# TensorE in source order in the second mixer, and a finer-stepped spectral mixing

## The chip, the cores and the metric

The kernel runs on one core of a Trainium2 chip. The time is device microseconds of one execution. The kernel before took 2022.99 us (median of 3 runs, 2015.35 to 2023.32). A core has TensorE (PE, with weight loads as PEld), VectorE (DVE), ScalarE (ACT), GpSimd (POOL) and SyncE (SP), whose queue issues nearly all DMAs here. Each engine works through its own queue in order, and engines wait for each other by semaphores.

## The reference

Attention over pooled keys and values, then a mixer with a low-rank mixing of the tokens, then a second mixer whose token mixing is the real part of a two-dimensional Fourier transform:

```python
attn_out = softmax(q @ pooled_k.T / 8) @ pooled_v      # 8 x 8 heads x 576 x 64
u  = x + (x.T @ U @ V).T                               # first mixer, 8 x 576 x 512
x1 = u + relu(u @ w_ch1) @ w_ch2                       # 512 -> 2048 -> 512
u2 = x1 + real(fft(fft(x1, axis=1), axis=2))           # second mixer
un = (u2 - mean(u2)) / sqrt(var(u2) + 1e-6)
out = u2 + relu(un @ moe2_w_ch1) @ moe2_w_ch2
```

All matrix products are made from pairs of rounded halves (high and low), so each is three matmuls.

## The kernel before

**The stages.** The first mixer works on 18 blocks of 256 tokens (16 slots a block); beside it run generators, called lanes, each of which does a little work per `step`: attention for the coming sequences, the conversion of the weights, and, once these are done, lane `d`, the spectral mixing of the eight sequences (`Dft.run`, in groups of 1, 2, 3 and 2 sequences). The second mixer works on 9 blocks of 512 tokens with 8 passes a block, called pairs here, since each takes two 128-column groups of the hidden layer: 72 pairs. Between its parts a `tick` steps all lanes, four times a pair. Lane `p` (`prep_a`) prepares the next block: it loads four tiles `ul` of the mixed sums, normalizes them (statistics on DVE, L762), transposes them on PE (L775), and splits them into operands `x`.

**A pair.** The first product of the mixer is made in seven sub-products of 256 x 256 x 256 (`product`, six matmuls of 256 columns each), of tiles `wr`, which hold two products each and come through a ring of four tiles from DRAM (`ring_load`). They go to the two halves of PSUM banks `h0` (`u`) and `h1` (`y`, `v`). In source order: s1 into `v`, a11 into `u`, s2 added to `u`, s4 added to `v`, a12 into `y`, s3 added to `u`, a22 added to `u`. ACT copies a half to `side` whenever the value so far is needed (L1157, L1159, L1166: s1, a11, and a11 + s2). DVE then adds `side` to both halves of `h1` (L103), ACT makes `hh` (relu, L1139) and DVE `hl` (L1140): that is the low half of the hidden layer; the high half follows from s3 and a22. `st2_a` multiplies these by the second weight: a group of six matmuls of 512 columns for each of four token tiles, into banks `o0`, `o1`, `hu`, `m`. Tiles 0 and 1 need the low half of the same pair, tiles 2 and 3 the high half of the pair before.

**A sequence of the spectral mixing.** For each of three row ranges it loads `F` and `R` (SP), forms sums and differences on POOL (`S`) and DVE (`R`, `E`), and splits them on ACT (`xh`, `xe`) and DVE. Then come five groups of matmuls with the table `st`, and two or three with `dt`, in banks `s0` and `s1`, with the sums stored to DRAM as `u2d`. Its `yield`s set how the work falls on steps: 17 a sequence, 19 for the last one of a group.

**What sets the order.** A scheduler orders PE, DVE, POOL and SP by a simulated timeline. ACT is in source order from the second block of the first mixer on (`order.enter_context`).

Of the kernel before, what the change touches and what calls it, by code (L numbers as in the profile page):

```python
# [38 lines left out]
NRING = 4  # L39
# [5 lines left out]
def kernel(  # L45
# [28 lines left out]
    mhalf = const.tile([128, 1], F32, name="mhalf")  # L74
    nc.vector.memset(mhalf, -0.5)
    W = {}
    state = {"n": 0, "free": False, "m": "s1", "u": 0, "slot": 0, "x1": 0, "u2": 0, "op": 0, "banks": ("s0", "s1", "hu")}

    def scratch(i, w=1024, dt=F32):

# [9 lines left out]
    def bank(tag):  # L90
        return ps_b.tile([128, 512], F32, tag=tag, name=tag)
# [10 lines left out]
    def add(eng, o, a, b):  # L102
        eng.tensor_tensor(out=o, in0=a, in1=b, op=ALU.add)  # L103
# [5 lines left out]
    def mm(o, a, b, start, stop):  # L109
        nc.tensor.matmul(o, a, b, start=start, stop=stop, skip_group_check=True)  # L110
# [393 lines left out]
    class Dft:  # L504
# [12 lines left out]
            self.cat = None  # L517

        def pbank(self):
            self.n += 1  # L520
            return bank(state["banks"][self.n % len(state["banks"])])

        def run(self, b, group):
            p1 = self.p
            z = b * S
            slot = b - group[0]

            def tl(tag, shape=(128, DM), dt=F32):
                return p1.tile(list(shape), dt, tag=tag, name=tag)
# [22 lines left out]
            fr = loads(0)  # L552
            yield
            yield
            X, XE = [], []
            for i in range(3):
                f, r, n = fr
                s = tl("S")
                e = tl("E")
                add(nc.gpsimd, s[:n], f[:n], r[:n])  # L560
                sub(nc.vector, r[:n], f[:n], r[:n])
                nc.gpsimd.tensor_copy(e[:n, 0:1], s[:n, 0:1])
                nc.gpsimd.memset(e[:n, 511:512], 0.0)
                sub(nc.vector, e[:n, 256:511], r[:n, 1:256], r[:n, 256:511])
                add(nc.vector, e[:n, 1:256], s[:n, 1:256], s[:n, 256:511])
                c2 = s[:n, 511:512].to_broadcast([n, 64])
                xe = tl(f"xe{i}", (128, 96 if i < 2 else 64), F32R)
                if i < 2:
                    xh, xl = tl(f"xh{i}", dt=F32R), tl(f"xl{i}", dt=F32R)
                    split(xh, xl, e)  # L570
                    nc.scalar.activation(out=xe[:, 0:64], in_=c2, func=ACTF.Copy)
                    sub(nc.vector, xe[:, 64:96], c2[:, 0:32], xe[:, 0:32].bitcast(F32))
                    X.append((xh, xl))
                    XE.append(xe)
                else:
                    m = self.sm
                    for h, y, w in ((xe, c2, 64), (None, e, 512)):
                        h = h or tl("S", dt=F32R)
                        q = r[:, 0:w]
                        nc.vector.tensor_scalar(out=q[:n], in0=y[:n], scalar1=m[:n, 0:1], scalar2=None, op0=ALU.mult)  # L580
                        nc.scalar.activation(out=h[:n], in_=y[:n], func=ACTF.Copy)
                        nc.vector.scalar_tensor_tensor(out=h[:n], in0=h[:n].bitcast(F32), scalar=m[:n, 1:2], in1=q[:n], op0=ALU.mult, op1=ALU.add)
                    X.append((h,))
                    XE.append(xe)
                    yield
                if i < 2:
                    fr = loads(i + 1)
                    yield
                yield
            P = []  # L590
            if slot == 0:
                self.cat = (tl("cath", (128, 4, 99), F32R), tl("catl", (128, 4, 99), F32R), tl("catp", (96, 99), F32R))
# [12 lines left out]
            for c in range(2):  # L605
                for g in range(2):
                    m = 127 if c and g else 128
# [17 lines left out]
            for i in range(3 if b == group[-1] else 2):  # L625
                f, r = tl("F"), tl("R")
                if i < 2:
                    k0, n = KT[i]
                    ks = slice(k0, k0 + n)
                    Q = [(ph[:m, ks], pl[:m, ks], m) for ph, pl, m in P]  # L630
                    qx = px[:, ks]
                    nc.sync.dma_start(out=f[:n], in_=x1d[z + k0:z + k0 + n, :])
                    mirror_in(r, i)
                else:
                    n = 33 * len(group)
                    hi, lo, qx = self.cat
                    Q = [(hi[:p[2], a, :n], lo[:p[2], a, :n], p[2]) for a, p in enumerate(P)]
                    qx = qx[:, :n]
                    for j, zj in enumerate(y * S for y in group):
                        nc.sync.dma_start(out=f[33 * j:33 * j + 33], in_=x1d[zj + 256:zj + 289, :])  # L640
                        nc.sync.dma_start(out=r[33 * j:33 * j + 32], in_=x1d[zj + 544:zj + 576, :])
                        nc.sync.dma_start(out=r[33 * j + 32:33 * j + 33], in_=x1d[zj + 288:zj + 289, :])
                yield
                yield
                a, bb = bank("s0"), bank("s1")
                for c, o in ((0, a), (1, bb)):
                    for g in range(2):
                        ph, pl, m = Q[2 * c + g]
                        th, tl_ = self.dt[:m, c, g, 0], self.dt[:m, c, g, 1]
                        last = c == 1 and g == 1  # L650
                        mm(o[:n, 0:NL], ph, th, g == 0, False)
                        mm(o[:n, 0:NL], ph, tl_, False, False)
                        mm(o[:n, 0:NL], pl, th, False, last)
                mm(a[:n, 0:NL], qx, self.pt, False, True)
                s, e = tl("S"), tl("E")
                nc.scalar.activation(out=e[:n, 0:NL], in_=bb[:n, 0:NL], func=ACTF.Copy)
                sub(nc.vector, s[:n, 0:257], a[:n, 0:257], e[:n, 0:257])
                add(nc.vector, e[:n, 0:257], a[:n, 0:257], e[:n, 0:257])
                add(nc.gpsimd, f[:n, 0:256], f[:n, 0:256], s[:n, 0:256])
                add(nc.vector, f[:n, 256:512], f[:n, 256:512], e[:n, 1:257])  # L660
                add(nc.vector, r[:n, 0:256], r[:n, 0:256], e[:n, 0:256])
                add(nc.gpsimd, r[:n, 256:512], r[:n, 256:512], s[:n, 1:257])
                if i < 2:
                    nc.sync.dma_start(out=u2d[z + k0:z + k0 + n, :], in_=f[:n])
                if i == 0:
                    for a, m in ((1, 15), (16, 112)):
                        nc.sync.dma_start(out=u2d[z + 288 + a:z + 288 + a + m, :], in_=r[a:a + m])
                elif i == 1:
                    nc.sync.dma_start(out=u2d[z + 416:z + 544, :], in_=r)
                else:  # L670
                    for j, zj in enumerate(y * S for y in group):
                        nc.sync.dma_start(out=u2d[zj + 256:zj + 289, :], in_=f[33 * j:33 * j + 33])
                        nc.sync.dma_start(out=u2d[zj + 544:zj + 576, :], in_=r[33 * j:33 * j + 32])
# [54 lines left out]
    def tbank():  # L728
        if state["free"] and len(pools) == 1:
            return bank("m")  # L730
        state["n"] += 1
        return bank(("s0", "s1")[state["n"] % 2])
# [11 lines left out]
    def prep_a(b):  # L744
# [11 lines left out]
        for t in range(TA // 128):  # L756
            u = us.pop(t)
# [12 lines left out]
            nc.vector.tensor_tensor(out=rs[:, 0:1], in0=rs[:, 0:1], in1=rs[:, 1:2], op=ALU.mult)  # L770
            nc.vector.tensor_scalar(out=u, in0=u, scalar1=mv[:, 0:1], scalar2=rs[:, 0:1], op0=ALU.subtract, op1=ALU.mult)
            yield
            o = tbank()
            for k in range(KD):
                nc.tensor.transpose(o[:, k * 128:k * 128 + 128], u[:, k * 128:k * 128 + 128], ident)  # L775
# [49 lines left out]
    def product(n, o, x, first):  # L825
        w = wring[n // 2][:, n % 2].rearrange("p h (k c) -> p h k c", k=2)
        for k in range(2):
            for a, y in ((0, 0), (0, 1), (1, 0)):
                mm(o, w[:, a, k], x[:, y, k], first and k == 0 and a == y == 0, False)
        if n % 2:  # L830
            del wring[n // 2]
            ring_load(n // 2 + NRING)

    def st1(js, f, tag):
        beside = len(js) == 1 and df is not None
# [136 lines left out]
    def step(name):  # L972
        g = lanes.get(name)
        if g is not None and next(g, 1):
            del lanes[name]
# [75 lines left out]
    for gi, js in enumerate(groups):  # L1051
# [5 lines left out]
        for f in range(NF):  # L1057
# [35 lines left out]
            for i in range(2 if wide else 1):  # L1093
                slot += 1
                if wide or slot % 4:
                    step("a")
                if slot % 4 != 3:
                    step("d")
                if prev and i < len(prev[0]):
                    st2(prev[0][i], prev[1], prev[2][i], tags[i])  # L1100
                for name in ("p", "mix", "w", "prep"):
                    step(name)
                if last:
                    step("p")
# [41 lines left out]
            step(name)  # L1146

    prev = None
    for b in range(NBA):
        for p in range(NPR):  # L1150
            x = ops[b]
# [46 lines left out]
            rest_a(b, t)  # L1198
    for t in range(2, TA // 128):
        st2_a(prev, t)  # L1200
    order.close()
    dbx.close()

# [101 lines left out]
```

## Time and profile before

| | |
|---|---|
| profiled execution | 2017.55 us |
| its span | 2015.8 us |
| PE busy, share of the span | 93% |
| PEld / DVE / ACT / POOL busy | 82% / 50% / 33% / 13% |
| granted PE clock, mean | 0.979 |
| DMA moved | 335.62 MB, mean 166 GB/s |

Busy times of matmuls overlap, since they are pipelined: a matmul of 256 columns shows 0.28 us and the next starts 0.12 us later. So the spacing of starts tells PE's pace, and the busy share doesn't. A releaser is what ended the idle time before an instruction, inferred from semaphore events; "issue" is put where the profile shows none.

### The profile page before, as it was taken

What the parts mean: (1) busy time and instruction counts of PE and PEld (TensorE: products, weight loads), DVE (VectorE), ACT (ScalarE), POOL (GpSimd) and SP (SyncE); (2) the same over time, 40 slices, a digit from 0 to 9 for tenths busy, and PEclk for the clock granted to TensorE, in tenths of its full rate; (3) what the DMA queues carried; (4) which work ended last, traced back from release to release, by engine and by line L of the source; (5) the groups of instructions that cost most, each with busy time, mean ns of one, the idle gap of its engine ahead of it and who ended that gap; (6) DMA issues with size and microseconds to landing.
All of it is one profiled execution on the core that took longest, in us unless ns stands there. A gap on an engine that the chain in (4) does not pass through costs nothing.

```text
span 2015.8 us, 30975 instructions
## 1 busy us (share of the span) xinstructions
PE 1874.7 (93%) x11252; PEld 1653.4 (82%) x11252; DVE 1002.7 (50%) x2285; ACT 674.7 (33%) x2116; POOL 258.5 (13%) x389
## 2 busy tenths in 40 slices
PE   4789999999999999999997898999999999998998
PEld 4578889888888888888886787888888888887887
DVE  7985464555544445455457545543434343434322
ACT  6553444344333322232234332322232323222321
POOL 3430111111100001112114312210000000000000
PEclk9799999999999999999999899999999999999999
DMA  9445464645635345223226556574656565656563
GB/s 362 154 135 152 139 213 131 195 156 165 194 106 154 92 138 146 76 65 104 79 82 217 191 167 234 196 240 157 209 170 207 166 206 179 191 177 198 166 221 126
DMA packets 255416, 335.62 MB, mean 166 GB/s; under 512 B 84576, under 2 KB 109248, under 8 KB 255264
## 3 DMA queue, kind: packets, MB, share of 16 engines
q1 hardware_dynamic: 254336, 330.25, 52.3%
q0 software_dynamic: 928, 3.40, 0.5%
q8 instruction: 89, 1.46, 0.3%
q14 instruction: 63, 0.52, 0.1%
HBM read 268.69 MB, written 64.88 MB: 165 GB/s over the span
## 4 chain that ended last, share of the span: by engine, by line
PE 63%; DMA 9%; DVE 5%; ACT 2%; issue 2%; POOL 1%; SPq 1%; DVEq 0%; POOLq 0%; ACTq 0%
PE h L110 29%; PE o L110 20%; PE hu L110 5%; PE m L110 4%; PE s L110 4%; DMA cv<-w2b 4%; DMA R<-x1d 1%; ACT side L1166 1%; DMA ud<-x 1%; DMA raw<-vr 1%; PE s L775 1%; DMA F<-x1d 1%; POOL S L103 0%; DVE hl L876 0%; ACT s L413 0%
## 5 line engine op out<-in xcount | busy, mean ns | idle before, releaser
L110 PE MATMUL h<-utx,w 128*128 128x256 f32 (+1 forms) x3048 | 477.6, 301 | 14.0 <-DVE hl L876 7.5
L110 PE MATMUL h<-x,wr 128*128 128x256 f32 x3024 | 430.3, 290 | 54.8 <-ACT side L1166 32.6
L110 PEld LDWEIGHTS h<-x,wr 128*128 128x128 f32 x3024 | 405.4, 194 | 89.1 <-ACT side L1166 46.1
L110 PEld LDWEIGHTS h<-utx,w 128*128 128x128 f32 x3048 | 431.1, 191 | 54.4 <-DVE hl L876 10.6
L110 PE MATMUL o<-w,hh 128*128 128x512 f32 x1632 | 473.4, 402 | 1.6 <-ACT hh L875 1.1
L110 PEld LDWEIGHTS o<-w,hh 128*128 128x128 f32 x1632 | 296.6, 192 | 53.2 <-ACT hh L875 2.7
L110 PE MATMUL o<-w,hl 128*128 128x512 f32 x816 | 268.9, 396 | 1.9 <-DVE hl L876 1.9
L103 DVE TENSOR_TENSOR side<-h,side 128x512 f32<-128x512 f32 (+1 forms) x144 | 79.2, 555 | 239.7 <-ACT side L1166 221.4
L110 PEld LDWEIGHTS o<-w,hl 128*128 128x128 f32 x816 | 148.0, 189 | 26.0 <-DVE hl L876 3.2
L1159 ACT ACTIVATE side<-h 128x256 f32<-128x256 f32 x72 | 27.6, 384 | 302.4 <-PE h L110 302.4
L413 ACT ACTIVATE s<-s,mx 128x72 f32<-128x72 f32 x296 | 90.7, 333 | 68.2 <-DVE mx L410 67.7
L870 ACT ACTIVATE low<-h 128x256 f32<-128x256 f32 x102 | 39.2, 384 | 218.5 <-PE h L110 162.4
L1139 ACT ACTIVATE hh<-side 128x512 fp32r<-128x512 f32 (+1 forms) x144 | 74.3, 521 | 81.2 <-DVE side L103 76.8
L100 DVE TENSOR_TENSOR x<-ul,x 128x256 fp32r<-128x256 f32 x112 | 43.6, 423 | 114.3 <-ACT x L106 114.3
L875 ACT ACTIVATE hh<-h 128x256 fp32r<-128x256 f32 x170 | 65.8, 387 | 94.9 <-PE h L110 86.3
L103 DVE TENSOR_TENSOR low<-h,low 128x256 f32<-128x256 f32 x102 | 42.9, 420 | 102.0 <-ACT hh L871 99.4
L876 DVE SCALAR_TENSOR_TENSOR hl<-h,hh 128x256 fp32r<-128x256 f32 x170 | 70.7, 416 | 32.6 <-ACT hh L875 32.0
L100 POOL TENSOR_TENSOR wo<-wo 128x256 fp32r<-128x256 f32 x56 | 43.4, 786 | 324.0 <-ACT wo L106 309.5
L766 POOL TENSOR_TENSOR rs<-mv,mhalf 128x1 f32<-128x1 f32 x36 | 20.9, 586 | 493.9 <-DVE mv L765 492.8
L110 PE MATMUL m<-w,hh 128*128 128x512 f32 x304 | 82.4, 390 | 0.0
L1140 DVE SCALAR_TENSOR_TENSOR hl<-side,hh 128x512 fp32r<-128x512 f32 (+1 forms) x144 | 77.6, 562 | 4.0 <-ACT hh L1139 3.5
L110 PE MATMUL hu<-w,hh 128*128 128x512 f32 x288 | 77.8, 392 | 1.3 <-ACT hh L1139 1.3
(254 smaller groups left out, 2446.9 us busy)
## 6 DMA issues: line engine op xcount, KB each, us to landing
wr<-wc SPq DMA_DIRECT2D x252, 512.0 KB
x<-x SPq DMA_DIRECT2D x56, 256.0 KB
wc<-wo SPq DMA_DIRECT2D x56, 256.0 KB
ur<-ud SPq DMA_DIRECT2D x36, 256.0 KB
x1d<-ur SPq DMA_DIRECT2D x36, 256.0 KB
ul<-u2d SPq DMA_DIRECT2D x36, 256.0 KB
ur<-u2d SPq DMA_DIRECT2D x36, 256.0 KB
out<-ur SPq DMA_DIRECT2D x36, 256.0 KB
```

What stands on the lines that cost most here:

```text
L100: eng.tensor_tensor(out=o, in0=a, in1=b, op=ALU.subtract)
L103: eng.tensor_tensor(out=o, in0=a, in1=b, op=ALU.add)
L110: nc.tensor.matmul(o, a, b, start=start, stop=stop, skip_group_check=True)
L413: nc.scalar.activation(out=s[:n, a], in_=v[:, k], func=ACTF.Exp, bias=mx[:n, a:a + 1], accum_out=sm[:n, a:a + 1])
L766: nc.gpsimd.tensor_tensor(out=rs[:, 0:1], in0=v, in1=mhalf, op=ALU.pow)
L775: nc.tensor.transpose(o[:, k * 128:k * 128 + 128], u[:, k * 128:k * 128 + 128], ident)
L870: nc.scalar.activation(out=low, in_=o[:, T:2 * T], func=ACTF.Copy)
L875: nc.scalar.activation(out=hh, in_=p, func=ACTF.Relu)
L876: nc.vector.scalar_tensor_tensor(out=hl, in0=p, scalar=0.0, in1=hh.bitcast(F32), op0=ALU.max, op1=ALU.subtract)
L1139: nc.scalar.activation(out=hh[:, i], in_=c, func=ACTF.Relu)
L1140: nc.vector.scalar_tensor_tensor(out=hl[:, i], in0=c, scalar=0.0, in1=hh[:, i].bitcast(F32), op0=ALU.max, op1=ALU.subtract)
L1159: nc.scalar.activation(out=side[:, 0], in_=u, func=ACTF.Copy)
```

## The change

Four edits. PE is put in source order from the start of the second mixer (`manual_schedule`). The spectral mixing gets more `yield`s (26 steps a sequence, 31 for the last of a group), asks for the next `F` and `R` one step ahead of the split, waits a step more ahead of the matmuls, and splits each last part in three steps; lane `d` is stepped in every slot of the first mixer instead of three of four. While a spectral sum is in banks `s0` and `s1`, a flag holds the transposes of lane `p` back, and both draw banks from one counter. `product` puts the request for a new weight tile one product later.

```diff
         def pbank(self):
-            self.n += 1
-            return bank(state["banks"][self.n % len(state["banks"])])
+            state["n"] += 1
+            return bank(state["banks"][state["n"] % len(state["banks"])])
...
             fr = loads(0)
+            yield
             yield
             yield
...
                 xe = tl(f"xe{i}", (128, 96 if i < 2 else 64), F32R)
+                if i < 2:
+                    fr = loads(i + 1)
+                yield
                 if i < 2:
                     xh, xl = tl(f"xh{i}", dt=F32R), tl(f"xl{i}", dt=F32R)
                     split(xh, xl, e)
...
                     yield
-                if i < 2:
-                    fr = loads(i + 1)
-                    yield
-                yield
+                yield
+            yield
...
                 yield
                 yield
+                yield
+                state["busy"] = True
                 a, bb = bank("s0"), bank("s1")
...
                 mm(a[:n, 0:NL], qx, self.pt, False, True)
+                yield
                 s, e = tl("S"), tl("E")
...
                 add(nc.gpsimd, r[:n, 256:512], r[:n, 256:512], s[:n, 1:257])
+                yield
+                state["busy"] = False
                 if i < 2:
                     nc.sync.dma_start(out=u2d[z + k0:z + k0 + n, :], in_=f[:n])
...
             yield
+            while state["busy"]:
+                yield
             o = tbank()
             for k in range(KD):
                 nc.tensor.transpose(o[:, k * 128:k * 128 + 128], u[:, k * 128:k * 128 + 128], ident)
...
                 mm(o, w[:, a, k], x[:, y, k], first and k == 0 and a == y == 0, False)
+        if state["late"] is not None:
+            ring_load(state["late"])
+            state["late"] = None
         if n % 2:
             del wring[n // 2]
-            ring_load(n // 2 + NRING)
+            state["late"] = n // 2 + NRING
...
-                if slot % 4 != 3:
-                    step("d")
+                step("d")
...
     prev = None
+    chain = ExitStack()
+    chain.enter_context(tc.manual_schedule(engines={mybir.EngineType.PE}))
     for b in range(NBA):
```

How rows move. PE in the middle of the sixth block, before: the first six-matmul rows of `h0` are a11; those of `h1` with `x2_16728` and `x2_16196` are s4 and a12; `h0` with `x2_16694` is s2, with `x2_16474` s3, with `x2_16363` a22; `h1_17340` is the next pair's s1. `hu`, `m` and `o0` are the groups of the second product.

```order
L110 MATMUL h0_17225<-x2_16193,wr_17110 128x256 x6
L110 MATMUL hu_16898<-w_771,hl_17205 128x512
L110 MATMUL hu_16898<-w_841,hl_17205 128x512
L110 MATMUL h1_17226<-x2_16728,wr_17144 128x256 x6
L110 MATMUL h1_17226<-x2_16196,wr_17159 128x256 x6
L110 MATMUL m_16937<-w_771,hl_17205 128x512
L110 MATMUL m_16937<-w_841,hl_17205 128x512
L110 MATMUL h0_17225<-x2_16694,wr_17144 128x256 x6
L110 MATMUL h0_17225<-x2_16474,wr_17159 128x256 x6
L110 MATMUL h1_17340<-x2_16475,wr_17202 128x256 x6
L110 MATMUL h0_17225<-x2_16363,wr_17202 128x256 x6
L110 MATMUL o0_16854<-w_937,hh_17278 128x512 x2
```

PE in a pair of the seventh block, now: `h0` with `x2_17555` is s2, `h1` s4 and a12, `h0` with `x2_17335` s3.

```order
L110 MATMUL hu_17759<-w_423,hl_17729 128x512
L110 MATMUL hu_17759<-w_469,hl_17729 128x512
L110 MATMUL h0_17741<-x2_17555,wr_17676 128x256 x6
L110 MATMUL h1_17742<-x2_17587,wr_17691 128x256 x6
L110 MATMUL h1_17742<-x2_17057,wr_17691 128x256 x6
L110 MATMUL m_17796<-w_423,hh_17728 128x512 x2
L110 MATMUL m_17796<-w_469,hh_17728 128x512 x2
L110 MATMUL m_17796<-w_423,hl_17729 128x512
L110 MATMUL m_17796<-w_469,hl_17729 128x512
L110 MATMUL h0_17741<-x2_17335,wr_17726 128x256 x6
L110 MATMUL o0_17713<-w_488,hh_17792 128x512 x2
L110 MATMUL o0_17713<-w_488,hl_17793 128x512
```

Between s2 and s3 there are now two products and a group of six wide matmuls, where there was nothing.

DVE at the end of the fifth block, before: the residual adds of that block (`ur`), the statistics of the next block's first two tiles (BN_STATS), and the add of `side` of the pair that runs then.

```order
L103 TENSOR_TENSOR ur_16781<-hu_16039,ur_16781 128x512
L762 BN_STATS bs_16977<-ul_16905 128x6
L103 TENSOR_TENSOR ur_16783<-m_16078,ur_16783 128x512
L762 BN_STATS bs_17073<-ul_16907 128x6
L763 BN_AGGR mv_16978<-bs_16977 128x2
L103 TENSOR_TENSOR side_11744<-h1_16786,side_11744 128x512
```

DVE at the same place, now.

```order
L103 TENSOR_TENSOR ur_16781<-hu_16041,ur_16781 128x512
L103 TENSOR_TENSOR side_11609<-h1_16786,side_11609 128x512
L769 BN_STATS bs_16977<-ul_16907 128x6
L769 BN_STATS bs_17073<-ul_16909 128x6
L103 TENSOR_TENSOR ur_16783<-m_16078,ur_16783 128x512
L770 BN_AGGR mv_16978<-bs_16977 128x2
L1151 SCALAR_TENSOR_TENSOR hl_16836<-side_11609,hh_16835 128x512
```

The add of `side` has gone ahead of the two statistics instructions; the `hl` that follows it stands behind them.

## Rows read from the trace of the kernel before

**Rows 1.** Busy times by window: span, engines with counts, PE clock, DMA share, GB/s

```profile
1350.00:2012.00 662.00, 622.49 (x3763) 551.92 (x3762) 247.99 (x609) 176.43 (x442) 14.10 (x24) 0.98 0.58 185
1550.00:1600.00 50.00, 48.54 (x299) 43.09 (x298) 19.34 (x48) 13.97 (x34) 1.10 (x2) 1.00 0.53 166
```

**Rows 2.** PE's waits, 1093 to 2016 us: total us, times, longest us

```profile
PE h L110 <- ACT side L1166: 32.6, 56, 7.0
PE h L110 <- issue: 14.6, 6, 3.2
PE s L110 <- DVE S L582: 6.9, 1, 6.9
PE s L110 <- ACT xh L106: 3.8, 1, 3.8
PE h L110 <- DVE low L103: 2.5, 1, 2.5
```

**Rows 3.** Timeline of a steady pair: start us, us, engine line op [idle before <-releaser]

```profile
1519.85 2.48 PE L110 MATMUL h<-x,wr 128*128 128x256 f32 x18 [0.47 <-ACT side L1166]
...
1522.17 2.00 PE L110 MATMUL o<-w,hh 128*128 128x512 f32 x8
...
1526.73 1.36 PE L110 MATMUL h<-x,wr 128*128 128x256 f32 x10
1527.92 0.63 PE L110 MATMUL hu<-w,hl 128*128 128x512 f32 x2
...
1529.80 0.86 PE L110 MATMUL h<-x,wr 128*128 128x256 f32 x6
1530.70 0.38 ACT L1166 ACTIVATE side<-h 128x256 f32<-128x256 f32 x1 [1.58 <-PE h L110]
...
1531.13 1.70 PE L110 MATMUL h<-x,wr 128*128 128x256 f32 x12 [0.47 <-ACT side L1166]
```

**Rows 4.** Groups by form, 1350 to 2000 us: count | busy us, mean ns | idle before

```profile
L1140 DVE SCALAR_TENSOR_TENSOR hl<-side,hh 128x512 fp32r<-128x512 f32 x55 | 38.0, 692 | 0.8 <-ACT hh L1139 0.4
L103 DVE TENSOR_TENSOR side<-h,side 128x512 f32<-128x512 f32 x55 | 37.9, 688 | 202.9 <-ACT side L1166 202.9
L1139 ACT ACTIVATE hh<-side 128x512 fp32r<-128x512 f32 x55 | 34.8, 632 | 54.4 <-DVE side L103 53.5
...
L775 PE MATMUL s<-ident,ul 128*128 128x128 f32 x96 | 13.4, 272 | 0.0
```

**Rows 5.** Timeline at the end of a block

```profile
1631.87 1.26 SPq L929 DMA_DIRECT2D out<-ur  x2
...
1635.01 0.93 SPq L750 DMA_DIRECT2D ul<-u2d  x2
...
1637.61 0.69 DVE L762 BATCH_NORM_STATS2 bs<-ul 128x6 f32<-128x512 f32 x1 [0.86 <-DMA ul<-u2d]
...
1638.81 0.68 DVE L762 BATCH_NORM_STATS2 bs<-ul 128x6 f32<-128x512 f32 x1
...
1639.49 0.99 DVE L103 TENSOR_TENSOR side<-h,side 128x512 f32<-128x512 f32 x2
...
1640.25 1.67 PE L110 MATMUL h<-x,wr 128*128 128x256 f32 x12 [1.62 <-issue]
```

**Rows 6.** Timeline of a spectral sequence beside the second mixer

```profile
1140.05 1.09 SPq L537 DMA_DIRECT2D R<-x1d  x3
...
1147.62 0.63 ACT L106 ACTIVATE xh<-E 128x512 fp32r<-128x512 f32 x1 [7.78 <-DVE E L100]
...
1148.72 4.21 PE L110 MATMUL h<-x,wr 128*128 128x256 f32 x18 [6.95 <-ACT side L1166]
...
1154.20 0.63 ACT L106 ACTIVATE xh<-E 128x512 fp32r<-128x512 f32 x1 [2.62 <-DVE E L100]
...
1162.43 0.63 ACT L581 ACTIVATE S<-E 99x512 fp32r<-99x512 f32 x1 [1.51 <-DVE R L580]
```

More of the change, by code (lines that the diff above doesn't have):

```diff
@@ L76 @@
     W = {}
-    state = {"n": 0, "free": False, "m": "s1", "u": 0, "slot": 0, "x1": 0, "u2": 0, "op": 0, "banks": ("s0", "s1", "hu")}
+    state = {"n": 0, "free": False, "m": "s1", "u": 0, "slot": 0, "x1": 0, "u2": 0, "op": 0, "busy": False, "late": None, "banks": ("s0", "s1", "hu")}
     def scratch(i, w=1024, dt=F32):
@@ L1200 @@
         st2_a(prev, t)
+    chain.close()
     order.close()
```

## The prediction

> **What bounds the kernel now.** I read the busy shares by window first, then TensorE's list of waits, then the timeline at the places which that list names. The windows [rows 1] split the second mixer in two. From 1350 us on it is periodic: 56 of its 72 pairs in 662 us, with TensorE busy for 622 of them, VectorE for 248 and ScalarE for 176, and the DMA engines at 58%. So TensorE's own work and its waits set the pace there, and nothing else is near full. Before 1350 us the same pairs share TensorE with the last spectral sequences. The list of waits [rows 2] has one large entry: 56 waits, 32.6 us, for ScalarE's copy `side` (L1166), then 14.6 us under "issue", then single long ones (6.9, 3.8, 2.5 us).
>
> The timeline of one pair [rows 3] shows what the 56 are. TensorE ends six matmuls of `h`, ScalarE copies that result from 1530.70 to 1531.08, and only then do the next matmuls of `h` start, at 1531.13: 0.47 us idle. In the order of before the s2 product is followed at once by the s3 product, which adds to the same PSUM half; s3 has to wait until s2's value has been copied out. It costs more than 0.47 us. A pair lasts 11.28 us (1519.85 to 1531.13). Ten matmuls of 256 columns take 1.19 us (1526.73 to 1527.92), 0.119 each. From 1522.17 to 1529.80, 7.63 us, there are 24 matmuls of 512 columns and 18 of 256: 18 x 0.119 = 2.14, so 24 take 5.49, 0.229 each. A pair of 42 and 24 without a wait is 5.00 + 5.49 = 10.49 us. So each wait costs 0.79 us: the idle time, the last matmul's drain and the slow restart.
>
> The "issue" waits are no issue. At the end of a block [rows 5] VectorE holds two statistics instructions that need the next block's `ul`, asked for at 1635.01 and used at 1637.61; the add of `side` sits behind both, at 1639.49, and TensorE's products, which overwrite what that add reads, start at 1640.25. VectorE's queue is the cause.
>
> The long waits are the spectral mixing [rows 6]: `R` is asked for at 1140.05, the sums of it are ready for ScalarE's `xh` at 1147.62 after 7.78 us of waiting, the copy of `side` stands behind it on ScalarE, and TensorE starts at 1148.72 after 6.95 us idle.
>
> **The change, part by part.** *TensorE in source order.* Between s2 and s3 there now stand s4, a12 and the group of six wide matmuls (the second fence of the rows above). At 0.714 us a product and 1.37 us a group that is 2.8 us of work over a copy of 0.38 us. The wait goes; what is late next? Count a pair from s1's start: s1 0.71, a11 1.43, group 2.80, s2 3.52, s4 4.23, a12 4.94, group 6.32, s3 7.03, group on the low half from 7.03. Its data come from the add of `side` after a12, then `hh`, then `hl`: 0.69, 0.63 and 0.69 us [rows 4]. With 0.2 us of drain and hand-offs, `hh` is there at 6.55 and `hl` at 7.25, and they are wanted at 7.03 and, four matmuls later, at 7.95. The slack is 0.5 and 0.7 us; so I cost the steady pair at 10.49.
>
> Steady part: 56 x 10.49 = 587 us, and at most 13 us for 96 transposes [rows 4], of which I take 10, since their busy times overlap: 597 of the 662 us. 65 us are lost now (some 50 pair waits of 0.79, the 14.6, and slow clock behind them). Left over afterwards: the block ends. On VectorE the add of `side` now stands ahead of the statistics, but the second statistics instruction stands ahead of `hl` (the fourth fence). The store of the residual tile that `ul` replaces was asked for at 1631.87 and its `ul` was in use at 1637.61, 5.7 us later [rows 5]. In the new order the second store follows the group that ends a pair, so it leaves about 1.0 us into the next and its statistics can run at 6.9 to 7.6; a residual add (0.69) and an aggregate follow, and `hl` ends at 9.2 instead of 7.95: 1.3 us, with the restart 2 us. Its bounds are 0 and the 3.2 us of the longest "issue" wait. Seven ends x 2 = 14 us, and 6 us for short waits that I can't place (one a block). 597 + 20 = 617: **45 us less**. If the slack is an illusion, the end for this term is no gain at all; if nothing is left over, 65.
>
> *More and later spectral steps.* A sequence takes 26 to 31 steps where it took 17 to 19. In the first mixer they are now taken in every slot instead of three of four, beside a TensorE without a gap (there I expect 0, either way a few us). In the second mixer a step comes four times a pair, every 2.62 us. The chain of [rows 6] is 7.6 us from request to the first `xh`, 6.6 to the second (1154.20), 8.2 to the third stage (1162.43): 22.4 us. ScalarE now meets these three at four, two and two steps after the request: 10.5, 15.7 and 21.0 us. The first two are covered, the third is 1.5 us late, and later if the request leaves late. The last sequence now ends in pair 29 instead of pair 15 by the program's order, but the one for which a block's preparation is held ends in pair 15 and is wanted in pair 22 at the latest, so no step is forced. I charge 3 us for each of four sequences (bounds: 0, and 22 if TensorE stands through the whole chain). 1093 to 1350 us is 257 us: 16 pairs are 168, the spectral matmuls (123 of 290 and 130 of 258 columns, at 0.119 x columns/256) 32, transposes and the first mixer's tail 8; 49 are lost. Afterwards: 9 at the transition (the 6.9 and 2.5 of [rows 2], whose chain the change leaves), 2 in the first pair, which has no earlier groups to put between, 12 for the sequences, 4 for two block ends, 8 for restarts and slow clock: 35. **14 us less.**
>
> *Weight tiles one product later.* A tile's slot is free when its second product ends and is wanted again about 9.7 us later (freed at 1.43, wanted at 11.2 in the count above). A 256 KB tile was asked for and in use within 2.6 us [rows 5]; twice the bytes should need at most 5.2. Behind the request on SP stand `ul`, stores and spectral loads, which gain when SP does not stand still for TensorE. I take 0 (bounds: 0, and what the rival below gives). *The flag that holds transposes back and the shared bank counter:* 0; it delays transposes that are wanted a block later.
>
> The clock. Behind the idle 6.95 us, 18 products took 4.21 us [rows 6] where 18 took 2.48 [rows 3]: 1.2 GHz for part of them. The 0.47 us waits do not do this: 1550 to 1600 us, with one in each pair, has a granted clock of 1.00 [rows 1]. The Trainium skill, "TensorE: Matmul & The Clock Gate", section "A second HAM failure mode: psum-queue depth-cycling", says otherwise: short idles between groups of matmuls, if frequent enough, make the clock swing. By that rule part of the steady pairs would run at 1.2 GHz now, and if it were a tenth of the 662 us another 33 us would come back, some 1928 us. The row decides; I count no clock for the short waits.
>
> **Sum.** 45 + 14 = 59 us off the profiled execution's own 2017.55: 1958.5. That execution lay 5.4 us under the median of the runs shown (2022.99, lowest 2015.35); with half of that, **1961 us**.
>
> **The rivals.**
> 1. *The wait moves to the low half.* The slack of 0.5 us goes to ScalarE's and VectorE's other work (splits of 0.4 us in order before `hh` or `hl`). For it: both queues are in order, and the block ends show it. Against: only some pairs have such work. With 0.5 us in each of 50 pairs, 25 us: 1986.
> 2. *It goes further.* The sequences cost nothing and the block ends vanish: 12 + 8 + 14, less 6 for what else appears: 1933.
> 3. *Weight tiles come late.* If a tile lands over 9.7 us after its slot is free, each of 252 waits; 0.2 us each is 50 us, the whole gain: 2011. Against: the DMA engines are at 58%.
> 4. *Slower: a convoy.* No scheduler puts other products ahead of a stalled one any more. SP's queue is in order: a spectral load stands behind weight tiles that wait for TensorE, which waits for `side`, which on ScalarE waits behind `xh` for that load. If a request leaves over three steps (8 us) late, all later stages are exposed: 22 us in each of four sequences, 88, with 2 us of slow clock at each of three stops 24: 112 where I charge 12 and 8. 1961 + 92 = 2053. For it: the 7.78 us for which ScalarE stood before `xh` [rows 6] are of this kind. Against: SP's order puts the loads a few tiles apart, and each tile ahead is free within a step.
>
> **How the numbers follow.** Forecast 0.65 (its own range 1940 to 1978), rival 1 0.16, rival 2 0.09, rival 3 0.04, rival 4 0.06. Under 0.5%, 10 us, a measurement of this kernel tells nothing from no change. Faster: 0.65 + 0.16 + 0.09 = 0.90; within: 0.04; slower: 0.06. The range for 8 in 10 takes in rival 1 and most of rival 2: 1935 to 2000.
>
> **What would show it.** Right: no wait for `side` in steady pairs, pairs of 10.5 us, the block ends' wait moved from the products to the `hl` matmuls. Spectral step: ScalarE's waits before the first two `xh` gone, one of a few us at the third. Wrong: a wait for `hh` or `hl` in every pair (rival 1), waits for `wr` on TensorE (3), TensorE idle over 5 us at each sequence (4).

## The result, and the profile after

The changed kernel takes 1967.9 us (median of 4 runs, 1965.5 to 1970.9) where the kernel before takes 2020.4 beside it: ratio 0.974, 95% interval 0.972 to 0.977. It is faster, 7 us above the predicted 1961 and inside the forecast's own range (1940 to 1978). The profiled execution took 1968.2 us, its span is 1966.4.

Windows of the changed kernel, columns as in [rows 1]:

```profile
1350.00:1962.00 612.00, 597.76 (x3724) 536.24 (x3724) 258.35 (x610) 183.08 (x444) 28.05 (x55) 0.99 0.63 198
1550.00:1600.00 50.00, 50.00 (x315) 44.97 (x314) 19.03 (x43) 17.25 (x43) 0.00 (x0) 1.00 0.55 172
```

From 1350 to 1962 us TensorE is idle for 14 us of 612, where it was idle for 39.5 of 662 [rows 1]. A window of steady pairs is full.

TensorE's waits in the changed kernel, 1080 to 1967 us (in all, times, longest), the counterpart of [rows 2]:

```profile
PE o L110 <- ACT hh L1150: 12.8, 8, 6.0
PE h L110 <- ACT side L1172: 8.6, 2, 5.1
PE o L110 <- DVE hl L1151: 5.6, 4, 1.9
PE h L110 <- DVE rs L776: 4.6, 3, 3.8
PE h L110 <- DVE hl L1151: 3.2, 1, 3.2
```

The 56 waits for `side` are gone; two long ones of that name are left, both beside the first pair or a spectral sequence. What remains is few and single. A steady pair, against [rows 3]:

```profile
1596.96 1.60 PE L110 MATMUL h<-x,wr 128*128 128x256 f32 x12
1598.40 1.09 PE L110 MATMUL hu<-w,hh 128*128 128x512 f32 x4
1599.33 0.62 PE L110 MATMUL hu<-w,hl 128*128 128x512 f32 x2
1599.79 2.32 PE L110 MATMUL h<-x,wr 128*128 128x256 f32 x18
...
1607.53 1.60 PE L110 MATMUL h<-x,wr 128*128 128x256 f32 x12
```

No row has an idle time in brackets. From start to start a pair takes 10.57 us (1596.96 to 1607.53; 11.28 before). Twelve matmuls of 256 columns (two products) pass in 1.44 us, a group of six wide ones in 1.39.

The end of the same block, against [rows 5]:

```profile
1611.35 0.93 SPq L757 DMA_DIRECT2D ul<-u2d  x2
...
1614.92 1.35 DVE L769 BATCH_NORM_STATS2 bs<-ul 128x6 f32<-128x512 f32 x2 [1.46 <-DMA ul<-u2d]
...
1616.87 0.66 DVE L1151 SCALAR_TENSOR_TENSOR hl<-side,hh 128x512 fp32r<-128x512 f32 x1
...
1617.58 0.73 PE L110 MATMUL o<-w,hl 128*128 128x512 f32 x2 [1.89 <-DVE hl L1151]
...
1619.03 1.91 PE L110 MATMUL o<-w,hh 128*128 128x512 f32 x4
```

VectorE stands 1.46 us for `ul`, then does two statistics, and only then `hl`, for which TensorE's `hl` matmuls have waited 1.89 us. The wait has moved from the products to these matmuls, as forecast. The last row shows the price on top: four wide matmuls in 1.91 us instead of 1.09.

A spectral sequence, against [rows 6]:

```profile
1225.80 0.31 SPq L545 DMA_DIRECT2D R<-x1d  x1
...
1230.36 1.26 POOL L103 TENSOR_TENSOR S<-F,R 99x512 f32<-99x512 f32 x1 [4.06 <-DMA R<-x1d]
1231.65 0.26 ACT L585 ACTIVATE xe<-S 99x64 fp32r<-99x64 f32 x1 [5.52 <-POOL S L103]
...
1234.64 4.21 PE L110 MATMUL h<-x,wr 128*128 128x256 f32 x18 [5.14 <-ACT side L1172]
```

This is the third load of the sequence, in six small pieces of `R`. ScalarE stands 5.52 us for its sum, the copy of `side` stands behind it, and TensorE idles 5.14 us. Before, it was the first load that did this.

### The profile page after: what moved, and what is told of

It is laid out like the page before. It is cut to its first block, busy times and chain, and to the rows that moved or that the text cites. A ratio compares the mean times of both kernels' runs of the same rounds, so it can differ in the third digit from the quotient of the medians.

```text
span 1966.4 us, 31064 instructions
## 1 busy us (share of the span) xinstructions
PE 1855.6 (94%) x11252; PEld 1642.8 (84%) x11252; DVE 1013.4 (52%) x2285; ACT 684.2 (35%) x2116; POOL 254.5 (13%) x389
## 3 DMA queue, kind: packets, MB, share of 16 engines
q8 instruction: 89, 1.46, 0.3%
## 4 chain that ended last, share of the span: by engine, by line
PE 62%; DMA 11%; DVE 6%; issue 1%; ACT 1%; SPq 1%; POOL 0%; DVEq 0%; POOLq 0%; ACTq 0%
PE h L110 27%; PE o L110 20%; PE hu L110 5%; PE s L110 4%; PE m L110 4%; DMA cv<-w2b 4%; DMA ul<-u2d 2%; DMA out<-ur 2%; DMA ud<-x 1%; DMA raw<-vr 1%; PE s L784 1%; DMA R<-x1d 0%; DMA wr<-wc 0%; DVE hl L888 0%; DVE bs L769 0%
## 5 line engine op out<-in xcount | busy, mean ns | idle before, releaser
L110 PE MATMUL o<-w,hh 128*128 128x512 f32 x1632 | 482.3, 400 | 14.6 <-ACT hh L1150 12.8
L110 PE MATMUL h<-x,wr 128*128 128x256 f32 x3024 | 419.2, 287 | 19.7 <-ACT side L1172 8.6
L110 PEld LDWEIGHTS o<-w,hh 128*128 128x128 f32 x1632 | 287.8, 190 | 61.1 <-ACT hh L1150 14.4
L110 PE MATMUL o<-w,hl 128*128 128x512 f32 x816 | 281.8, 398 | 7.9 <-DVE hl L1151 5.6
L413 ACT ACTIVATION_READ_ACCUMULATOR s<-s,mx 128x1 f32 x296 | 64.1, 217 | 0.0
L110 PEld LDWEIGHTS s<-v,e 128*128 128x128 f32 x370 | 59.3, 194 | 5.7 <-ACT e L421 1.5
```

What stands on the lines that cost most here:

```text
L413: nc.scalar.activation(out=s[:n, a], in_=v[:, k], func=ACTF.Exp, bias=mx[:n, a:a + 1], accum_out=sm[:n, a:a + 1])
```

## The experiments

All ratios are to the kernel before, run beside on the same chip. The time of a pair is read from start to start of VectorE's 128x512 add of `side`, which comes once in each pair.

**e1, the order alone.** To the kernel before, only:

```diff
+    chain.enter_context(tc.manual_schedule(engines={mybir.EngineType.PE}))
     for b in range(NBA):
```

> The kernel before with one edit: TensorE keeps the order of the source in the second mixer. Spectral steps, the shared counter and the weight requests stay as before. Theory A (the order alone takes the wait out of the steady pairs; finer steps only soften the sequences): the steady pairs fall from 11.28 to about 10.57 us as in the changed kernel, 2020 - 45; the coarse steps let ScalarE meet the three loads of a sequence 2.4, 1.4 and 3.0 us early (two steps of 2.62 us against 7.6, 6.6 and 8.2 us), 6.8 us in each of four sequences, 27, with restarts 4, against some 16 in the changed kernel: about 1983 us (1975 to 1995). Rival B (the gain is not the order but SP's queue and the later requests): about 2020. Rival C (a convoy: without finer steps TensorE stands through whole chains): 2040 or more, with idle times over 5 us at each of the four sequences.

1989.6 us, 0.985 (0.983 to 0.986): 31 us less, inside theory A's range. Steady pairs take 10.56 us. The first 16 pairs take 238 us where they took 237, so beside the coarse sequences the fixed order neither gained nor lost; the gain lies in the pairs behind them. Rivals B and C fall.

**e2, the spectral steps alone.** The changed kernel without `manual_schedule` for TensorE and with the weight tile asked for at once.

> The changed kernel without the order for TensorE and with weight tiles asked for at once: what is left is the spectral mixing in more and later steps, the flag, the shared counter. Theory A: the wait for the copy of side stays in every steady pair (0.47 us idle, 11.28 us a pair), and the finer steps give at most the 14 us of the prediction's second term: 2006 to 2020 us. Rival B (finer steps are the gain, the order is not): under 1985.

2002.2 us, 0.991 (0.990 to 0.993): 18 us less. Its waits:

```profile
PE h L110 <- ACT side L1174: 28.2, 56, 3.1
PE h L110 <- issue: 10.3, 5, 2.5
```

The 56 waits stand as before and its steady pairs still take 11.28 us; rival B falls. The gain is 4 us over theory A's most.

**e3, weight tiles at once.** To the changed kernel:

```diff
-            state["late"] = n // 2 + NRING
+            ring_load(n // 2 + NRING)
```

> The changed kernel with one edit taken back: a weight tile is asked for right behind its second product, not one product later. Theory A: a tile has about 9.7 us from free to wanted either way, so 1968 us, 4 us either way. Rival: the request stands on SP until TensorE has ended the product, and ul, stores and spectral loads behind it leave later; then the block ends and the sequences get longer and the time is 1976 or more.

1969.1 us, 0.976 (0.973 to 0.978), against 0.974: no difference that can be told. This run holds order and steps without the later requests, so the two edits can be added: 0.0153 + 0.0089 = 0.0242, together 0.0244. They act on different waits.

**e4, s3 right behind s2**, with TensorE in source order:

```diff
             product(n + 2, u, x["s2"], False)
             nc.scalar.activation(out=side[:, 1], in_=u, func=ACTF.Copy)
+            product(n + 5, u, x["s3"], False)
+            add(nc.vector, side[:, 2], u, side[:, 2])
             product(n + 3, v, x["s4"], False)
             product(n + 4, y, x["a12"], False)
...
-            product(n + 5, u, x["s3"], False)
```

The bookkeeping that frees a weight tile follows the new order of the products (not shown).

> The changed kernel with TensorE still in source order, but the source puts the s3 product right behind the s2 product again (s1, a11, s2, s3, s4, a12, a22), with the add of side behind it. The result is the same. Theory A (it is this one neighbourhood that costs): the wait of 0.47 us for the copy of side is back in every pair, each pair is 0.71 us longer (11.28 against 10.57), about 66 pairs, 47 us: 2010 to 2020 us, as before the change. Rival B (any fixed order gives the gain, or it comes from other queues): under 1980.

2040.2 us, 1.011 (1.008 to 1.013): slower than the kernel before, 20 us over theory A's range. Its waits:

```profile
PE h L110 <- ACT side L1183: 38.5, 72, 1.0
PE o L110 <- ACT hh L1154: 22.2, 7, 7.0
```

The wait for `side` is back, once in each of 72 pairs, so the neighbourhood is the cause and rival B falls. The miss has a place: a steady pair takes 11.70 us, not 11.28. Without s3 between, the low half's group comes 0.71 us earlier, and `hh` is not ready. First the rows of a steady pair in the changed kernel, then those of one in this run:

```profile
1602.93 0.63 ACT L1150 ACTIVATE hh<-side 128x512 fp32r<-128x512 f32 x1
1604.04 1.09 PE L110 MATMUL o<-w,hh 128*128 128x512 f32 x4
...
1666.95 0.76 PEld L110 LDWEIGHTS o<-w,hh 128*128 128x128 f32 x4 [0.56 <-ACT hh L1154]
1666.95 1.20 PE L110 MATMUL o<-w,hh 128*128 128x512 f32 x4
```

In the changed kernel `hh` ends at 1603.56, 0.48 us before the matmuls that read it. In this run they start 0.05 us behind its end in most pairs, and the weight load shows the wait. So the slack in the changed kernel is about 0.4 us (0.48 less 0.05; the prediction said 0.5). Of the 0.71 us some 0.3 are then late, and with four matmuls in 1.20 us instead of 1.09 that is about the 11.70 - 11.28 = 0.42 us. 72 x 0.42 is 30 us, which covers the miss.

**e5, VectorE in source order too.**

```diff
-    ...engines={mybir.EngineType.PE}
+    ...engines={mybir.EngineType.PE, mybir.EngineType.DVE}
```

> The changed kernel with one edit more: in the second mixer VectorE, too, keeps the order of the source, so that the statistics of the next block stand behind hl and not ahead of it. Theory (what the steady pairs of 10.57 us leave over are the block ends on VectorE's queue): a block without spectral work takes 89 to 90 us in the changed kernel, 8 x 10.57 and some 1.4 us of transposes are 86, so up to 4 us at each of seven ends, and the same queue costs waits beside the sequences: 15 to 25 us less, 1943 to 1953 us, with no wait of TensorE for hl after 1520 us. Rival: in source order VectorE stands at every sum whose R has not come, with side, hl and the statistics behind it, and the sequences get longer by what the ends save: 1966 us or more.

1975.2 us, 0.975 (0.973 to 0.977): no gain, the rival's time. The waits for `hl` after 1520 us are gone, and these stand instead, in each block:

```profile
1591.76 0.97 PE L110 MATMUL h<-x,wr 128*128 128x256 f32 x6 [0.80 <-DVE side L103]
...
1612.27 1.20 PE L110 MATMUL o<-w,hh 128*128 128x512 f32 x4 [0.53 <-ACT hh L1150]
```

A block without spectral work takes 89.0 us, against 88.8 to 90.2. Other work of VectorE for the next block now stands ahead of the add of `side`, in other pairs: three differences of `ul`, 1.34 us together, ahead of the first wait shown, and two splits, 0.76 us, ahead of the second. Both are longer than the slack of 0.4 us. The other half of the rival, longer sequences, is seen too: the first 32 pairs take 424.8 us, 413.2 in the changed kernel (one execution of each).

**e6, the third sum one step later.** To the changed kernel:

```diff
+                if i == 2:
+                    yield
                 add(nc.gpsimd, s[:n], f[:n], r[:n])
```

> The changed kernel with one step more in each sequence, ahead of the sums of the third load (the largest number of steps added there for which no preparation is forced). Theory (ScalarE meets the third load of a sequence too early, as at 1228 us, where it stood 5.52 us for it): 2.6 us less at each of two or three sequences, with the slow clock behind them 5 to 9 us in all: 1959 to 1964 us. Rival: the wait moves on to the next stage, or the lag is SP's, which issues the pieces of R late: 1968 us, 3 us either way.

1964.3 us, 0.970 (0.968 to 0.972) against 0.974 for the changed kernel: 9 us by the ratios, at the upper end of the theory (this chip was slower throughout: before 2027). The two intervals overlap by a hair, so the size is loose. The waits of 5.14 and 3.84 us are gone; the longest in the second mixer is 2.8 us.

**e7, e5 and e6 together.**

> The edits of the two runs before together. If they act on different waits (block ends; third load), their gains add up: 1936 to 1948 us by the theories, 1968 by the rivals. If VectorE's order costs at the sequences, the added step gives more here than alone.

1970.5 us, 0.973 (0.971 to 0.975): VectorE's order gives nothing here either. It seems to take back most of what the added step gave (the intervals of e6 and e7 just overlap).

**e8, the order, and a spectral step in every slot, with coarse steps.** To e1:

```diff
-                if slot % 4 != 3:
-                    step("d")
+                step("d")
```

> The kernel before with TensorE in source order and a spectral step in every slot of the first mixer (three of four before), but the coarse steps of before, the old counter, no flag, weights at once. It splits the second term: theory A (finer steps matter because ScalarE meets the loads later): the pace alone leaves the waits of the order-alone run, 1980 to 1990 us. Rival B (the gain of the steps is only that more of the spectral work is done when the second mixer begins): 1965 to 1975 us.

1981.0 us, 0.978 (0.976 to 0.980): 0.0068 below the order alone, some 14 us. As it stands, 1981 lies in theory A's range, but this chip was slower. Where the kernel before takes 2020 us it is 1975, the upper edge of rival B, and theory A expected at most 9 us. In the traces 132 of the 544 spectral matmuls come behind the second mixer's first product, 231 in e1. So 99 have moved, about one and a half sequences of 68. e3, which has the finer steps, flag and counter besides (and weights at once, as here), lies another 0.0023 lower (5 us; the intervals overlap), although 264 spectral matmuls come in the second mixer there.

**e9, six buffers for `ul` and `ur`**, on top of e6:

```diff
-  bufs=2 if len(pools) == 1 else 4
+  bufs=2 if len(pools) == 1 else 6
```

> The third-sum-later kernel with six instead of four buffers for ul and ur in the second mixer, so that the first ul tiles of a block need not wait for the stores of the block before. In the built order the first two statistics now stand ahead of the residual adds of the block before, half a pair earlier, not ahead of hl. Theory (the block end costs what it does because ul comes late and its statistics stand ahead of hl): the first pair of a block falls from 13.4 to 14.3 us to 10.6 to 11.6, some 2.5 us at each of seven ends, 17 us: about 1947 to 1955 us on a chip where the changed kernel takes 1968. Rival (VectorE's extra work of a block, some 9 us, meets a slack of half a us wherever it stands, as in the run with VectorE in source order, whose blocks took 89.0 us too): the waits move into other pairs, 1960 to 1967 us.

1954.3 us, 0.966 (0.964 to 0.968): the fastest of all, 66 us under the kernel before. But the theory is half wrong. One block end:

```profile
1593.93 1.50 DVE L771 BATCH_NORM_STATS2 bs<-ul 128x6 f32<-128x512 f32 x2 [1.23 <-DMA ul<-u2d]
...
1595.35 0.41 DVE L1153 SCALAR_TENSOR_TENSOR hl<-h,hh 128x256 fp32r<-128x256 f32 x1
...
1595.82 0.98 PE L110 MATMUL h<-x,wr 128*128 128x256 f32 x6 [1.03 <-DVE hl L1153]
...
1604.42 0.73 PE L110 MATMUL o<-w,hl 128*128 128x512 f32 x2 [1.05 <-DVE hl L1153]
```

The scheduler used the earlier load to put the statistics earlier too, and VectorE still waits 1.23 us for `ul` with `hl` behind it. One wait became two smaller ones, in the last pair of a block and the first of the next (12.0 and 11.9 us, where they took 10.6 and 13.4 to 14.3). Blocks without spectral work save about 1 us; the rest of the gain lies before 1520 us, and which wait it is there was not settled. Over e6 the gain is 0.0035, some 7 us. The two intervals just overlap; that of e10, which has e6's edit without the buffers and ran on the same chip as e9, does not reach e9's.

**e10 and e11, the normalisation on GpSimd**, on top of e6 and of e9 (L778):

```diff
-            nc.vector.tensor_scalar(out=u, ...
+            (nc.gpsimd if len(pools) > 1 else nc.vector).tensor_scalar(out=u, ...
```

> The third-sum-later kernel with the normalisation of ul (L778 of the changed kernel, 0.55 us on VectorE, four a block) on GpSimd in the second mixer. Theory (ul late and the statistics ahead of hl are the block end): no change, 1960 to 1967 us, because the normalisation is not what stands ahead of hl. Rival (it is VectorE's amount of work that meets the slack): each of some 32 normalisations spares up to 0.5 us, 8 to 15 us less.

> Both edits: six buffers for ul and ur, and the normalisation on GpSimd. If late ul is the cause, as six buffers alone (1947 to 1955 us); if VectorE's amount of work is, some 10 us below six buffers alone.

1960.9 us, 0.970 (0.968 to 0.972), no change; with six buffers 1959.2, 0.970 (0.968 to 0.971), rather a loss. GpSimd takes 2.1 us for what VectorE does in 0.55:

```profile
L780 POOL TENSOR_SCALAR ul<-ul,mv,rs 128x512 f32<-128x512 f32 x20 | 41.9, 2102 | 5.0 <-issue 2.5 <-DVE rs L779 1.4 <-DMA out<-ur 0.6
```

The fence is from e11. So the normalisation, one part of VectorE's work, is not what costs time at the block end, as far as a move to a slower engine can tell. The rows show what stands there: the statistics ahead of `hl`, waiting for `ul`. But what they cost is not shown by a gain. Without them ahead of `hl` (e5), and with an earlier load (e9), most of the time went into other waits.

**e12, more spectral work in the first mixer**, on top of e9:

```diff
                 step("d")
+                if slot % 2:
+                    step("d")
```

> The six-tiles kernel with a second spectral step in every other slot of the first mixer. By the built order 106 of the 288 spectral matmuls that stood in the second mixer now stand in the first, some one and a quarter sequences. Theory B (what the step edit gains is spectral work taken out of the second mixer: the run with a step in every slot and coarse steps moved 102 of its 240 and took 14 us less than the order alone): 10 to 16 us less than six tiles, ratio to the kernel before about 0.960, 1939 to 1946 us where six tiles takes 1954. Theory A (with fine steps a sequence costs the second mixer only its 3 to 4 us of waits, its matmuls take the same time on either side): 4 to 6 us less. Rival: two steps in a slot let ScalarE meet the loads early beside the first mixer, whose TensorE has no gap now: no gain or a loss, with TensorE below 50 of 50 us in the windows from 800 to 1050 us.

1959.0 us, 0.968 (0.966 to 0.970): no gain over 0.966. TensorE stays full beside the faster steps:

```profile
800.00:1050.00 250.00, 249.75 (x1349) 215.39 (x1348) 138.47 (x317) 75.48 (x222) 50.16 (x92) 1.00 0.33 93
```

So neither theory holds as put, and the rival's time came without its sign. By the traces 102 spectral matmuls moved (276 behind the second mixer's first product in e9, 174 here), and nothing came of it. The traces show the difference to e8 (one execution each). There the end of the first mixer, counted from the 2501st to the last of its 3048 matmuls `h<-utx,w`, grew by 10.4 us against e1, and all that comes behind shrank by 20.9. Here it grew by 9.4 us against e9, and what comes behind shrank by 10.5. With fine steps a sequence costs the second mixer little beyond its matmuls, which take their time on either side. In these runs moving sequences paid only while they were coarse.

## Why the prediction was right, step by step

**Steady pairs: right, mis-sized by 5 us.** The wait was the neighbourhood of s2 and s3 (e4 puts it back), and nothing took its place in a steady pair. The pair is 10.57, not 10.49 us: 24 wide matmuls take 5.56 us (four groups of 1.39), not 5.49. Rival 1 didn't come: in a steady pair `hh` and `hl` end 0.48 and 0.68 us ahead of their matmuls, as worked out (0.5 and 0.7; the prediction's own terms add up to 0.1 us more, since 4.94 + 0.69 + 0.63 + 0.2 is 6.46 and not 6.55). But it was near: one product less between eats the slack up (e4).

**The order's term: 45 predicted, 31 measured alone.** From the 17th pair's add of `side` to the last one e1 takes 614.3 us, where the kernel before takes 650.1: 35.8 us less, 9 short of the 45. The pair's 0.07 us makes 4 of these. The block ends make the rest: a block takes 90.1 us on average, 5.6 over eight pairs of 10.56, where the prediction allowed 4.3 (10 us of transposes, 14 of block ends and 6 unplaced, over seven blocks). The other 5 us lie ahead of the 17th pair, for which this term forecast nothing. The first 16 pairs took 1 us more. The rest is no larger than what executions differ by there: the first mixer, where e1 changes nothing, ended 6 us later in its profiled execution (1097.5 against 1091.1 us). In the changed kernel the ends are a little smaller (88.8 to 90.2 us a block): the wait for `hl` measured 1.1 to 1.9 us against the 1.3 worked out, and the unplaced part is a second wait one or two pairs later, for `hh`:

```profile
1706.96 0.73 PE L110 MATMUL o<-w,hl 128*128 128x512 f32 x2 [1.30 <-DVE hl L1151]
...
1717.52 1.20 PE L110 MATMUL o<-w,hh 128*128 128x512 f32 x4 [0.66 <-ACT hh L1150]
```

**The spectral term: 14 predicted, 18 measured alone; the reason holds for the change as built, but it is not the only way to the gain.** I put the whole gain on loads that are met later. In e2 276 spectral matmuls come behind the second mixer's first product, 243 in the kernel before, so the gain there is not work taken out of the second mixer. TensorE's idle time in it fell, from 69 to 56 us (its whole list of waits in both). What the prediction missed is the pace: of a step in every slot of the first mixer it said "there I expect 0", and gave it no part of the gain. With coarse steps the faster pace alone gave some 14 us on top of the order (e8), most likely because a coarse sequence costs nothing beside the first mixer (TensorE was busy there for 248.7 of the 250 us from 800 us on) and costs its waits beside the second. The finer steps seem to remove much the same waits a second way, since they add little where the pace is there already (e3 against e8). Finer steps at the old pace were not run.

The rest held in the main. The first two loads of a sequence cost TensorE 1 us or less at most places, but ScalarE's waits ahead of `xh` are not gone as the prediction wanted: up to 3.88 us, where they were up to 9.24. The third load was late, by up to 5.14 us of TensorE's time where I charged 3 a sequence. One first load was late too, 3.24 us at 1404.78.

**The transition: the sum right, the waits not.** 11 us were charged for it, on the chain of 6.9 and 2.5 us left as it is. The 6.9 us wait is gone, since another stage stands there now. In its place:

```profile
1095.15 1.76 PE L110 MATMUL h<-x,wr 128*128 128x256 f32 x11 [1.19 <-DVE x L100]
1100.36 4.37 PE L110 MATMUL h<-x,wr 128*128 128x256 f32 x24 [3.44 <-ACT side L1172]
1110.71 2.07 PE L110 MATMUL o<-w,hh 128*128 128x512 f32 x4 [5.98 <-ACT hh L1150]
```

With two of half a us these are 11.7 us, in the first pair, which has no groups to put between.

**Weight tiles: 0, right** (e3); there is no wait for `wr`. The flag and the shared counter, also put at 0, were not tried alone. Rivals 3 and 4 didn't come; not even coarse steps made a convoy (e1).

**The clock.** The windows at 1550 us show a granted clock of 1.00 with a 0.47 us wait in every pair [rows 1] and without one. So there the waits, when they went, gave back no clock. The rule weighed in the prediction (the Trainium skill, "TensorE: Matmul & The Clock Gate", section "A second HAM failure mode: psum-queue depth-cycling") has short idles make the clock swing when they are frequent; these windows don't show it, and the 33 us that the prediction put on it, if a tenth of the time were at 1.2 GHz, didn't come. (The 18 products in its comparison of clocks are 18 matmuls.)

**The sum.** Too much for the order (14 us) and too little for the steps (4 us): 59 predicted, 49 measured in the profiled executions. The two errors partly cancel, and the near hit of the total owes something to that.

## What to carry to other kernels

When an engine reads out what the next instruction overwrites, put other ready work between the two in the order; count the slack of whatever then comes last, because here it was 0.4 us: one product moved brought back a wait of 0.71 us a pair and cost 0.42 more, together more than the change had gained. Look for instructions that wait for a DMA in an in-order queue ahead of work on the critical chain. But don't count their wait as won: here more buffers split it in two, since the load was still used as soon as it was expected, and another order put other work in its place. Before finer steps and an earlier start are both built, ask whether they remove the same wait.

## What the runs showed of the hardware that was not expected

Waits of nearly one size had different prices. Two windows of the changed kernel around a block end:

```profile
1610.00:1625.00 15.00, 13.11 (x73) 11.32 (x72) 8.47 (x26) 2.58 (x6) 1.61 (x3) 0.89 0.77 255
1704.00:1720.00 16.00, 14.04 (x87) 12.15 (x86) 11.36 (x37) 3.17 (x9) 2.26 (x4) 1.00 0.73 232
```

The first holds one idle time of 1.89 us and has a granted clock of 0.89, part of it at 1.2 GHz: 15 x 0.11 = 1.65 us of full-speed work not done. The second holds idle times of 1.30 and 0.66 us at a clock of 1.00. A wait of 1.67 us at 1538.76 was also followed by four wide matmuls at full pace (1.20 us). What decides between them was not tried.
